# q of the first chunk, one token tile at a time

## The chip, the cores and the metric

The kernel runs on one core of a Trainium2 chip. The metric is the device time of one execution in microseconds (us). The core's engines each run their own queue of instructions in order and wait for one another through semaphores: TensorE (matmuls, and transposes as matmuls with an identity), VectorE, ScalarE, GpSimd, and SyncE (SP), which here only starts transfers. ScalarE and GpSimd can start transfers too. In the profile these are PE (weight loads apart, as PEld), DVE, ACT, POOL and SP; L284 is line 284 of the kernel.

## What is computed

One block of a transformer on x (2048 tokens, 1024 features): h = x + attention(layernorm(x)), then h2 = h + gated MLP(layernorm(h)). The change lies in the first projection of the first 512 tokens. Cut to it:

```
qkv = (layernorm(x) @ wqkv).reshape(B, S, 3, H, Dh)      # H = 32 heads of Dh = 32
logits = einsum('bhsd,bhswd->bhsw', q, kg) * scale       # 8 keys per token, 2 apart
o = einsum('bhsw,bhswd->bhsd', softmax(logits), vg)
h = x + o @ wo
h2 = h + B(layernorm(h))                                 # gelu, spatial mixing over all tokens, w_out
```

The layernorm has no learned scale: (x - mean) / sqrt(var + 1e-5), over the features of a token.

## The kernel before

The 2048 tokens are cut into 4 chunks of 512, and a chunk into 4 token tiles of 128 (one token per partition). Chunk 0 begins the kernel. Its tiles' statistics come from VectorE (`stats`, `stats_half`: two bn_stats of 512 columns and a bn_aggr) or, for tile 3, from two summing passes on ScalarE (`sums_act`, `var_act`). ScalarE takes the root, VectorE the reciprocal, and `norm` writes the normalised tile `xn`. TensorE transposes it in 8 blocks of 128x128 (`xpose`), because a matmul needs the features on the partitions, and two copies (`xput`) bring the transposed tile from PSUM, the accumulation memory, into `xnT[0]`. For tiles 0 and 2 the copies are ScalarE's, for 1 and 3 VectorE's.

The q projection multiplies `wqs`, the 1024x1024 weights of q, with `xnT[0]`. The contraction over 1024 features is cut into 8 slices (kt), the 1024 outputs into 8 groups of 128 (dl). `wqs` is seen with the dl index innermost, so the 128 weight columns of one dl lie 8 elements apart in memory; the same holds for k and v (`wk`, `wv`, L433), not for the weights of later stages (`win`, L790). Before, tiles 0 and 1 go together through q: for dl 0 to 3, all kt, 32 matmuls of 256 columns (`q_left`; 24 of them before the transposes of tiles 2 and 3, 8 after). Then tiles 2 and 3 do the same for dl 0 to 3, 32 matmuls of 256 columns; then all four tiles go through dl 4 to 7, 32 matmuls of 512 columns. All 96 are on L284. `q_out` copies finished accumulators into `att_in[0][0]`, from which attention reads q.

TensorE's clock is at half speed at first. Before any data is there, TensorE runs `NWARM` = 20 matmuls on zeros (L209).

PSUM holds three `acc` buffers and one `L` buffer. Transposed tiles 0 and 2 go through `L`, as do the warm-ups; 1 and 3 go through `acc`.

Transfers of the start: SP issues half of x0 and half of x1 (tiles 0 and 1), ScalarE the other halves, then SP all of x2 and ScalarE all of x3. GpSimd issues `csb`, the constants with the identity that the transposes need (104 KB). Then SP issues the 8 slices of wq (256 KB each), two pairs of x tiles for chunk 1, wk, x for chunks 2 and 3, and wv.

In this part of the kernel each engine's order is the order of the source, written by hand. The rest (k and v of chunk 0, the layernorm of chunks 1 to 3, attention, MLP) is ordered by a list planner, `Order`. It is given a cost in us for each operation and, in `Order({...})`, the time at which each engine is taken to become free after the hand-written part; it decides in which order operations are issued, not when. `G` keeps its operations. The planner's items on "DMA" with fixed times (17.5 for the sums of tile 7, 26.2 for q) stand for times at which something is taken to be ready.

After q, TensorE's next work is k of chunk 0 (L433), 64 matmuls of 512 columns, then v, and then it is filled by projections of later chunks while VectorE does attention.

Of the kernel before, what the change touches and what calls it, by code (L numbers as in the profile page):

```python
# [10 lines left out]
FP32 = mybir.dt.float32  # L11
BF16 = mybir.dt.bfloat16
# [8 lines left out]
P = 128  # L21
# [8 lines left out]
EPS = 1e-5  # L30
SCALE = DH ** -0.5
NEG = -1.0e9
NWARM = 20
XRB = 3
LMODE = (1, 1, 1, 1)
LSLACK, BSLACK = 2.0, 2.0
# [89 lines left out]
def kernel(  # L126
# [28 lines left out]

    cpool = ctx.enter_context(tc.tile_pool(name="consts", bufs=1))
    csb = cpool.tile([P, 416], BF16, name="csb")
    dma_w(csb[:], consts_d.ap()[:, :])
    ident = csb[:, 0:128]
    E32 = csb[:, 128:160]  # L160
    B4 = csb[:, 160:288]
# [17 lines left out]
    def new_acc():  # L179
        return ps_acc.tile([P, 2, CH], FP32, name="acc", tag="acc")  # L180
# [19 lines left out]
    def load_pair(k):  # L200
        x_slot(2 * k)
        x_slot(2 * k + 1)
        dma(pairs[k][:], x2d[2 * k * P:(2 * k + 2) * P, :].rearrange("(t p) d -> p t d", p=P))
# [10 lines left out]
    with tc.manual_schedule(engines={mybir.EngineType.SP}):  # L214
        for i in range(TPC):
            x_slot(i)
        for i in range(2):
            for q_, lo in ((nc.sync, 0), (nc.scalar, CH)):
                q_.dma_start(xts[i][:, lo:lo + CH], x2d[i * P:(i + 1) * P, lo:lo + CH])
        dma(xts[2], x2d[2 * P:3 * P, :])  # L220
        A.dma_start(xts[3], x2d[3 * P:4 * P, :])
        for kt in range(KT):
            dma(wsb[0][:, kt, :], wq_view[:, kt, 0:D])
        load_pair(2)
        load_pair(3)
        dma(wsb[1][:], wq_view[:, :, D:2 * D])
        load_pair(4)
        load_pair(5)
        xl = att.tile([P, TPC, D], BF16, name="xl", tag="prod", bufs=2)
        dma(xl[:], x2d[3 * CH:4 * CH, :].rearrange("(t p) d -> p t d", p=P))  # L230
        for i in range(TPC):
            xts[3 * TPC + i] = xl[:, i, :]
        dma(wsb[2][:], wq_view[:, :, 2 * D:3 * D])
# [4 lines left out]
        eng.bn_stats(st[:, 1, :], xts[i][:, 512:1024])  # L238
        V.bn_aggr(mv1[:, i, :], st[:])

    def stats_half(i, hf, st=None):
        if hf == 0:
            st = l1.tile([P, 2, 6], FP32, name="bnst", tag="bnst")
        V.bn_stats(st[:, hf, :], xts[i][:, hf * CH:(hf + 1) * CH])
        if hf:
            V.bn_aggr(mv1[:, i, :], st[:])
        return st

    def sums_act(i, k, junk, sm=None):
        if k == 0:  # L250
            sm = l1.tile([P, 4], FP32, name="sm", tag="sm")
        A.activation(junk, xts[i], (ACTF.Identity, ACTF.Square)[k], accum_out=sm[:, k:k + 1])
        return sm
# [6 lines left out]
    def root(lo, hi):  # L260
        sd = l1.tile([P, TPC], FP32, name="sd1", tag="sd1")
        A.activation(sd[:, 0:hi - lo], mv1[:, lo:hi, 1], ACTF.Sqrt, bias=eps_t[:])
        return sd

    def norm(i, out=None):
        xn = l1.tile([P, D], BF16, name="xn", tag="xn", bufs=4)[:] if out is None else out
        V.tensor_scalar(xn, xts[i], mv1[:, i, 0:1], rstd1[:, i:i + 1], op0=ALU.subtract, op1=ALU.mult)
        return xn

    xnT[0] = xtp.tile([P, TPC, KT, P], BF16, name="xnT", tag="xnT")  # L270

    xns = {c: bp.tile([P, TPC, D], BF16, name=f"xns{c}", tag=f"hn{c - 1}", bufs=1) for c in (1, 2)}

    def xpose(i, xn):
        tps[i] = ps_acc.tile([P, 2, 2 * CH], BF16, name="tpb", tag="acc") if i % 2 else ps_att.tile([P, 2, 2 * CH], BF16, name="tpa", tag="L")
        for a in range(KT):
            T.transpose(tps[i][:, a // 4, (a % 4) * P:(a % 4 + 1) * P], xn[:, a * P:(a + 1) * P], ident)  # L277

    def xput(i):
        for hf in range(2):  # L280
            (V.tensor_copy if i % 2 else A.copy)(xnT[0][:, i, 4 * hf:4 * hf + 4, :], tps[i][:, hf, 0:CH].rearrange("p (a s) -> p a s", a=4))  # L281

    def q_mm(dl, kt, lo, hi):
        T.matmul(qacc[dl // 2][:, dl % 2, lo * P:hi * P].rearrange("p (a b) -> p a b", b=P), wqs[:, kt, dl, :], xnT[0][:, lo:hi, kt, :],  # L284
                 start=(kt == 0), stop=(kt == KT - 1))

    def q_left(lo, hi):
        for kt in range(lo, hi):
            for dl in range(4):
                q_mm(dl, kt, 0, 2)  # L290

    def q_out(dp):
        A.copy(att_in[0][0][:, 2 * dp:2 * dp + 2, :], qacc[dp][:])

    att_in = {}

# [5 lines left out]
        alloc_att_in(0, which)  # L302
    V.memset(att_in[0][1][:, :, 0:HALO], 0.0)
    V.memset(att_in[0][2][:, :, 0:HALO], 0.0)
    tps, qacc = {}, {}
    wqs = wsb[0][:].rearrange("p kt (m dl) -> p kt dl m", dl=DLO)

    def junk():
        return l1.tile([P, D], BF16, name="jk", tag="xn", bufs=4)[:]

    wsq = l1.tile([P, 1], FP32, name="wsq", tag="wsq")
    A.activation(wsq[:], eps_t[:], ACTF.Sqrt)
    stats(V, 0)
    sd0 = root(0, 1)
    stats(V, 1)
    sd1 = root(1, 2)
    sm = sums_act(3, 0, junk())
    V.reciprocal(rstd1[:, 0:1], sd0[:, 0:1])
    xn = {0: norm(0)}
    V.reciprocal(rstd1[:, 1:2], sd1[:, 0:1])  # L320
    xn[1] = norm(1)
    xpose(0, xn[0])
    xput(0)
    st2 = stats_half(2, 0)
    xpose(1, xn[1])
    xput(1)
    stats_half(2, 1, st2)
    sums_act(3, 1, junk(), sm)
    sd2 = root(2, 3)
    var_act(3, sm)  # L330
    sd3 = root(3, 4)
    V.reciprocal(rstd1[:, 2:3], sd2[:, 0:1])
    xn[2] = norm(2)
    V.reciprocal(rstd1[:, 3:4], sd3[:, 0:1])
    xn[3] = norm(3)
    qacc[0], qacc[1] = new_acc(), new_acc()
    q_left(0, 6)
    xpose(2, xn[2])
    xput(2)
    xpose(3, xn[3])  # L340
    xput(3)
    q_left(6, KT)
    sm7 = sums_act(7, 0, junk())
    sums_act(7, 1, junk(), sm7)
    for dp in range(2):
        for dl in (2 * dp, 2 * dp + 1):
            for kt in range(KT):
                q_mm(dl, kt, 2, TPC)
        q_out(dp)
    for dp in (2, 3):  # L350
        qacc[dp] = new_acc()
        for dl in (2 * dp, 2 * dp + 1):
            for kt in range(KT):
                q_mm(dl, kt, 0, TPC)
        q_out(dp)
    wo_sb = wtile([P, DLO, D], "wo_sb", "wB")
    win_view = B_w_in.rearrange("(kt p) n -> p kt n", p=P)
    win_specs = [(FH, 1024), (FH + 1024, 768), (0, 1024), (1024, 768)]
# [4 lines left out]
        dma_w(t[:], win_view[:, :, c0:c0 + wd])  # L363
        wins[k] = t

    o_ = Order({"PE": 24.9, "ACT": 26.0, "DVE": 14.4, "POOL": 12.0}, {"acc": 3, "L": 1, "prod": 1, "part": 2, "xn": 4})
    add = o_.add
    G = {}

# [8 lines left out]
    def ln1(c):  # L378
        sts = []
        for il in range(TPC):  # L380
            i = c * TPC + il
            arrive = add("DMA", X_AT[c] + 0.8 * il, lambda: None)
            if il < TPC - 1 or c == 3:
                sts.append(add("DVE", 1.4, lambda i=i: stats(V, i), [arrive], prio=LNPRIO[c]))
                continue
            if c == 1:
                G["sm", c] = sm7
                sa = add("DMA", 17.5, lambda: None)
            else:
                def sums(i=i):  # L390
                    G["sm", c] = sums_act(i, 0, junk())
                    sums_act(i, 1, junk(), G["sm", c])
                sa = add("ACT", 2.4, sums, [arrive], prio=4.0, lat=0.2)
            sts.append(add("DVE", 0.45, lambda i=i: var_act(i, G["sm", c]), [sa], prio=LNPRIO[c]))
        def ve():
            G["ve", c] = l1.tile([P, TPC], FP32, name="ve1", tag="ve1")
            V.tensor_scalar(G["ve", c][:], mv1[:, c * TPC:(c + 1) * TPC, 1], EPS, None, op0=ALU.add)
        s1 = add("DVE", 0.15, ve, sts, prio=LNPRIO[c] - 0.5)
        r1 = add("POOL", 1.05, lambda: nc.gpsimd.tensor_tensor(rstd1[:, c * TPC:(c + 1) * TPC], G["ve", c][:], nhalf[:], op=ALU.pow),
                 [s1], lat=0.4)  # L400
        def nrm(il):
            if c == 3 and il == 0:
                xns[c] = bp.tile([P, TPC, D], BF16, name="xns3", tag="hn0", bufs=1)
            norm(c * TPC + il, xns[c][:, il, :])
        ns = [add("DVE", 0.48, lambda il=il: nrm(il), [r1] + ([G["xnT", 1]] if c == 3 else []), prio=LNPRIO[c] - 0.5,
                  free="prod" if c == 3 and il == TPC - 1 else None) for il in range(TPC)]
        G["normed", c] = ns[-1]
        def tr():
            xnT[c] = xtp.tile([P, TPC, KT, P], BF16, name="xnT", tag="xnT")
            i_ = nc.sync.dma_start_transpose(xnT[c][:].rearrange("p il a s -> p (il a) s"), xns[c][:].rearrange("s il (a p) -> s (il a) p", p=P))  # L410
            if c == 3:
                tc.add_manual_dep(i_.ins, G["vload", 1].ins.name, wait_for, reason="keep the xbar transpose out of the sums and loads")
        G["xnT", c] = dma_op(9.0, tr, ns + ([G["qkvlast", c - 2]] if c >= 2 else []))
# [40 lines left out]

    def attention(c):
        if c == 0:
            d_q = add("DMA", 26.2, lambda: None)
            d_k, d_v = G["ev", 0, 1, 3], G["ev", 0, 2, 3]
        else:
            def ld(which):  # L460
# [486 lines left out]
```

## Time and profile before

| | us |
|---|---|
| median of 3 runs | 727.18 (726.68 to 727.5) |
| the profiled execution | 727.23 |
| its span in the profile | 725.4 |
| TensorE busy in the span | 718.2 |
| first k matmul starts | 24.97 |
| first copy of tile 0 into xnT starts | 9.33 |
| VectorE's first work for chunk 1 starts | 14.77 |
| first product of attention (VectorE) starts | 40.03 |

The profile's span begins with the first instruction and ends with the last; the time of an execution has some 1.8 us around it. "Busy" of TensorE counts pipelined matmuls whose ends are modelled: a matmul of 512 columns shows 379 ns, but the next starts 216 ns after it. Where the starts of matmuls matter, they are read from the timeline. The granted clock of the profile's row PEclk is 9 (90% or more) in all of its 40 slices, but the profile's warm-up matmuls follow each other at 0.427 us until 6.72 us and at 0.216 us from 6.97 us on, so that the change of speed is read from them.

### The profile page before, as it was taken

To read this page: it belongs to the slowest core of one execution; us is meant where nothing else is said; L and a number is where in the kernel's file an instruction comes from. 1 tells how busy PE (TensorE), PEld (TensorE's weight loads), DVE (VectorE), ACT (ScalarE), POOL (GpSimd) and SP (SyncE) were. 2 spreads that over 40 slices of the span, in tenths; PEclk is the share of its full clock that TensorE was granted. 3 is DMA by queue.
4 is the path that set the end of the run, shared out by engine and by line. 5 is a ranking of instruction groups with operands and counts; after the bars stand their busy time and mean duration, and the time that the engine had idled before them with its cause. 6 is when DMAs were issued, how large, how long until landed. Compare 5 with 4: busy or idle time off the path is not lost.

```text
span 725.4 us, 8425 instructions
## 1 busy us (share of the span) xinstructions
PE 718.2 (99%) x3445; PEld 369.1 (51%) x3490; DVE 420.1 (58%) x467; ACT 224.7 (31%) x278; POOL 54.0 (7%) x62
## 2 busy tenths in 40 slices
PE   8999999999999999999999999999999999999998
PEld 6666665666545444444444444444444444444444
DVE  6899899989999899989940102222222222222222
ACT  4422522534338864769735520000000000000000
POOL 0100010112110110201203100000000000000000
PEclk9999999999999999999999999999999999999999
DMA  8955598488993594372759799254115311020002
GB/s 306 335 169 121 168 215 209 126 233 238 270 339 59 169 210 162 112 223 51 191 135 291 218 298 284 70 109 139 44 44 130 117 44 43 30 88 14 1 16 72
DMA packets 114614, 110.49 MB, mean 152 GB/s; under 512 B 67632, under 2 KB 92112, under 8 KB 114448
## 3 DMA queue, kind: packets, MB, share of 16 engines
q1 hardware_dynamic: 105504, 72.63, 35.2%
q0 software_dynamic: 8496, 36.74, 17.8%
q10 hardware_dynamic: 576, 0.59, 0.2%
q8 instruction: 27, 0.44, 0.2%
q14 instruction: 11, 0.09, 0.0%
HBM read 55.09 MB, written 30.74 MB: 118 GB/s over the span
## 4 chain that ended last, share of the span: by engine, by line
PE 99%; issue 0%; DVE 0%
PE acc L886 27%; PE acc L433 21%; PE acc L790 13%; PE acc L740 13%; PE acc L901 13%; PE acc L667 8%; PE acc L284 2%; PE wps L209 1%; PE pb L576 0%; PE L L521 0%; PE tpa L277 0%; PE tpb L277 0%; DVE xnT L281 0%; DVE ot L915 0%; DVE warm L206 0%
## 5 line engine op out<-in xcount | busy, mean ns | idle before, releaser
L886 PE MATMUL acc<-wspT,z2sb 128*128 128x512 bf16 x878 | 193.1, 379 | 0.9
L886 PEld LDWEIGHTS <-z2sb 128*128 128x128 bf16 x896 | 87.7, 98 | 105.7
L889 DVE TENSOR_TENSOR g<-acc,bB 128x1024 bf16<-128x1024 f32 x28 | 34.3, 1224 | 160.1 <-PE acc L886 128.2
L740 PE MATMUL acc<-win,hnT 128*128 128x512 bf16 (+1 forms) x500 | 97.7, 352 | 0.6
L790 PE MATMUL acc<-hnT,win 128*128 128x512 bf16 x448 | 98.0, 379 | 0.0
L740 PEld LDWEIGHTS <-hnT 128*128 128x128 bf16 x512 | 49.8, 98 | 47.6 <-issue 0.9
L491 DVE TENSOR_TENSOR prod<-qT,kT 128x4096 bf16<-128x4096 bf16 x32 | 72.6, 2286 | 0.5 <-ACT kT L439 0.5
L901 PEld LDWEIGHTS <-zg 128*128 128x128 bf16 x462 | 45.2, 98 | 51.7
L790 PEld LDWEIGHTS <-win 128*128 128x128 bf16 x448 | 43.6, 98 | 52.6 <-issue 0.9
L908 DVE TENSOR_TENSOR ot<-acc,hr 128x1024 bf16<-128x1024 f32 x15 | 18.4, 1225 | 69.4 <-PE acc L901 60.5
L901 PE MATMUL acc<-wout_a,zg 128*128 128x512 bf16 (+1 forms) x260 | 58.0, 372 | 0.3
L444 ACT CAST stg<-acc 128x1024 bf16<-128x1024 f32 x36 | 36.4, 1012 | 70.1 <-PE acc L433 62.2
L433 PE MATMUL acc<-xnT,wk 128*128 128x512 bf16 x256 | 56.5, 379 | 0.0
L433 PE MATMUL acc<-xnT,wv 128*128 128x512 bf16 x256 | 56.3, 379 | 0.0
L667 PE MATMUL acc<-wo_sb,av_oT 128*128 128x512 bf16 x250 | 55.6, 379 | 0.3
L433 PEld LDWEIGHTS <-wk 128*128 128x128 bf16 x256 | 36.5, 144 | 19.0 <-issue 0.7
L433 PEld LDWEIGHTS <-wv 128*128 128x128 bf16 x256 | 36.6, 144 | 18.7 <-issue 0.5
L901 PE MATMUL acc<-wout_b,zg 128*128 128x512 bf16 (+1 forms) x193 | 43.8, 372 | 0.2
L433 PE MATMUL acc<-xnT,wq 128*128 128x512 bf16 x192 | 42.4, 380 | 0.0
L667 PEld LDWEIGHTS <-av_oT 128*128 128x128 bf16 x256 | 25.0, 98 | 30.1
L495 DVE TENSOR_TENSOR prod<-prod 128x2048 bf16<-128x2048 bf16 x32 | 38.5, 1220 | 0.0
L747 ACT ACTIVATE u<-acc 128x1024 bf16<-128x1024 f32 (+1 forms) x32 | 29.3, 916 | 29.0 <-PE acc L740 28.7
(142 smaller groups left out, 573.8 us busy)
## 6 DMA issues: line engine op xcount, KB each, us to landing
qkv_d<-stg SPq DMA_DIRECT2D x36, 256.0 KB, 3.5
z_d<-z1s SPq DMA_DIRECT2D x28, 256.0 KB, 2.6
z1c<-z_d SPq DMA_DIRECT2D x28, 256.0 KB, 3.1
z_d<-u SPq DMA_DIRECT2D x12, 448.0 KB, 3.2
z2sb<-z_d POOLq DMA_DIRECT2D x12, 448.0 KB, 10.2
xr<-in_A_x_dram SPq DMA_DIRECT2D x16, 256.0 KB, 2.7
av_y<-av_z POOLq DMA_DIRECT2D x4, 1024.0 KB, 9.2
av_oT<-av_zz POOLq DMA_DIRECT2D x4, 1024.0 KB, 12.0
```

What stands on the lines that cost most here:

```text
L433: T.matmul(G[key][:, j, :].rearrange("p (a b) -> p a b", a=TPC), wv[:, kt, dl, :], xnT[c][:, :, kt, :], start=(kt == 0), stop=(kt == KT - 1))
L444: A.copy(stg[:], G[key][:])
L491: V.tensor_tensor(st["prod"][:], qT[:], kT[:, :, o:o + CH], op=ALU.mult)
L495: V.tensor_tensor(dst, p_[:, 0:4, :], p_[:, 4:8, :], op=ALU.add)
L667: T.matmul(st["acc", il][:, nh, :], oTs[c][:, dl, il * P:(il + 1) * P], wo_sb[:, dl, nh * CH:(nh + 1) * CH], start=(dl == 0), stop=(dl == ...
L740: T.matmul(accf[:, n0:n1], hnTs[c][:, il, kt, :], wins[hf][:, kt, n0:n1], start=(kt == 0), stop=(kt == KT - 1))
L747: A.activation(st["u", il][:, hf * 1024:hf * 1024 + wd], G["accz", c, il, hf][:].rearrange("p a b -> p (a b)")[:, 0:wd], ACTF.Gelu_apprx_t ...
L790: T.matmul(G["accy", c, fp][:, j, :].rearrange("p (a b) -> p a b", a=TPC), wt[:, kt, f0 * P:(f0 + 1) * P], hnTs[c][:, :, kt, :], start=(kt ...
L886: T.matmul(acc[:, j, :], z2sb[a][:, f * P:(f + 1) * P], wspT[:, a, :], start=(a == 0), stop=(a == NT - 1))
L889: V.tensor_tensor(g1[:], acc[:], bB[:, c * CH:(c + 1) * CH].unsqueeze(1).to_broadcast([P, 2, CH]), op=ALU.add)
L901: T.matmul(outs, zg[:, f, il * P:(il + 1) * P], wt[:, f0, lo:hi], start=(f == 0), stop=(f == NF - 1))
L908: V.tensor_tensor(ot[:], acc[:].rearrange("p a b -> p (a b)"), hr[:], op=ALU.add)
```

## The change

Chunk 0's q is cut by token tile. Tile 0 goes alone through all 8 slices and all 8 dl (64 matmuls of 128 columns, `q_tile(0, ...)`), tile 1 the same (64), and then tiles 2 and 3 together (64 matmuls of 256 columns in two halves of four dl). Transposes and copies are issued by half tiles (4 blocks). The copies of tiles 0 and 1 are ScalarE's, those of 2 and 3 VectorE's. The two halves of tile 0 use an `acc` and the `L` buffer, tile 1 an `acc`, tiles 2 and 3 `L`. Statistics of all four tiles are VectorE's, each tile with its own root, reciprocal and norm in turn; tile 0's norm is made in two halves. x2 and x3 are issued by SP behind wq slices 3 and 5. `csb` is issued by ScalarE, between its halves of x0 and x1. There are 14 warm-up matmuls, not 20. Four times given to the planner are changed, and one more by 0.1.

```diff
-NWARM = 20
+NWARM = 14
...
-    dma_w(csb[:], consts_d.ap()[:, :])
...
         for i in range(2):
             for q_, lo in ((nc.sync, 0), (nc.scalar, CH)):
                 q_.dma_start(xts[i][:, lo:lo + CH], x2d[i * P:(i + 1) * P, lo:lo + CH])
-        dma(xts[2], x2d[2 * P:3 * P, :])
-        A.dma_start(xts[3], x2d[3 * P:4 * P, :])
+            if i == 0:
+                A.dma_start(csb[:], consts_d.ap()[:, :])
         for kt in range(KT):
             dma(wsb[0][:, kt, :], wq_view[:, kt, 0:D])
+            if kt in (3, 5):
+                i = 2 + kt // 4
+                dma(xts[i], x2d[i * P:(i + 1) * P, :])
...
+    def tp_tile(in_l):
+        pool, tag = (ps_att, "L") if in_l else (ps_acc, "acc")
+        return pool.tile([P, 2, 2 * CH], BF16, name="tp" + tag, tag=tag)
+
+    def xpose(i, hf, ps):
+        for a in range(4):
+            T.transpose(ps[:, hf, a * P:(a + 1) * P], xn[i][:, (4 * hf + a) * P:(4 * hf + a + 1) * P], ident)
+
+    def xput(i, hf, ps, cp):
+        cp(xnT[0][:, i, 4 * hf:4 * hf + 4, :], ps[:, hf, 0:CH].rearrange("p (a s) -> p a s", a=4))
+
+    def q_mm(dst, dl, kt, lo, hi, first=True, last=True):
+        T.matmul(dst.rearrange("p (a b) -> p a b", b=P), wqs[:, kt, dl, :], xnT[0][:, lo:hi, kt, :],
+                 start=(first and kt == 0), stop=(last and kt == KT - 1))
+
+    def q_tile(i, lo, hi):
+        if lo == 0:
+            qacc[i] = new_acc()
         for kt in range(lo, hi):
-            for dl in range(4):
-                q_mm(dl, kt, 0, 2)
+            for dl in range(DLO):
+                q_mm(qacc[i][:, dl // 4, (dl % 4) * P:(dl % 4 + 1) * P], dl, kt, i, i + 1, dl % 4 == 0, dl % 4 == 3)
+
+    def q_tile_out(i):
+        A.copy(att_in[0][0][:, :, i * P:(i + 1) * P], qacc[i][:].rearrange("p a (d s) -> p (a d) s", d=4))
...
+    def scale(i):
+        sd = root(i, i + 1)
+        V.reciprocal(rstd1[:, i:i + 1], sd[:, 0:1])
...
     stats(V, 0)
+    scale(0)
+    xn[0] = norm(0, parts=2)
+    tpa, tpl = tp_tile(False), tp_tile(True)
+    xpose(0, 0, tpa)
+    xput(0, 0, tpa, A.copy)
+    xpose(0, 1, tpl)
+    xput(0, 1, tpl, A.copy)
     stats(V, 1)
+    scale(1)
     xn[1] = norm(1)
+    q_tile(0, 0, 4)
+    tp = tp_tile(False)
+    xpose(1, 0, tp)
+    xpose(1, 1, tp)
+    q_tile(0, 4, 6)
+    xput(1, 0, tp, A.copy)
+    stats(V, 2)
+    scale(2)
     xn[2] = norm(2)
+    xput(1, 1, tp, A.copy)
+    q_tile(1, 0, 4)
+    stats(V, 3)
+    scale(3)
     xn[3] = norm(3)
+    tp = tp_tile(True)
+    xpose(2, 0, tp)
+    xpose(2, 1, tp)
+    xput(2, 0, tp, V.tensor_copy)
+    xput(2, 1, tp, V.tensor_copy)
+    q_tile(0, 6, KT)
+    q_tile_out(0)
+    tp = tp_tile(True)
+    xpose(3, 0, tp)
+    xpose(3, 1, tp)
+    xput(3, 0, tp, V.tensor_copy)
+    xput(3, 1, tp, V.tensor_copy)
+    q_tile(1, 4, KT)
     sm7 = sums_act(7, 0, junk())
+    q_tile_out(1)
     sums_act(7, 1, junk(), sm7)
+    for half in range(2):
+        acc = new_acc()
+        for j in range(4):
             for kt in range(KT):
+                q_mm(acc[:, j // 2, (j % 2) * 2 * P:(j % 2 + 1) * 2 * P], 4 * half + j, kt, 2, TPC)
+        A.copy(att_in[0][0][:, 4 * half:4 * half + 4, 2 * P:CH], acc[:].rearrange("p a (d s) -> p (a d) s", d=2))
...
-    o_ = Order({"PE": 24.9, "ACT": 26.0, "DVE": 14.4, "POOL": 12.0}, {"acc": 3, "L": 1, "prod": 1, "part": 2, "xn": 4})
+    o_ = Order({"PE": 22.4, "ACT": 23.6, "DVE": 14.5, "POOL": 12.0}, {"acc": 3, "L": 1, "prod": 1, "part": 2, "xn": 4})
...
-                sa = add("DMA", 17.5, lambda: None)
+                sa = add("DMA", 17.8, lambda: None)
...
-            d_q = add("DMA", 26.2, lambda: None)
+            d_q = add("DMA", 23.9, lambda: None)
```

## The prediction

> **What bounds the kernel.** I read the page's totals first, then the chain of waits in order of time, then the waits of TensorE alone. The totals (busy us, share of the span, instructions):
>
> ```profile
> PE 718.2 (99%) x3445; PEld 369.1 (51%) x3490; DVE 420.1 (58%) x467; ACT 224.7 (31%) x278; POOL 54.0 (7%) x62
> ```
>
> The chain (start, length, what):
>
> ```profile
> 1.19 7.25 PE wps L209 x20
> 8.45 0.04 issue
> 8.49 0.61 PE tpa L277 x8
> 9.09 0.46 PE tpb L277 x8
> ...
> 9.58 0.43 DVE xnT L281
> ...
> 10.15 2.81 PE acc L284 x24
> 12.96 0.45 PE tpa L277 x8
> 13.41 0.45 PE tpb L277 x8
> 13.85 11.28 PE acc L284 x72
> 25.14 50.07 PE acc L433 x232
> ```
>
> The waits of TensorE that are not for the warm-ups, all of them (sum, times, longest):
>
> ```profile
> PE acc L284 <- DVE xnT L281: 0.6, 1, 0.6
> ```
>
> TensorE works without a break from 10.15 us to the end; the chain behind 25.14 holds nothing but its matmuls and 0.05 us gaps. So what the change is worth is the moment at which the first k matmul (L433) starts: 24.97 us by the timeline. Up to there TensorE has 20 warm-ups (until 8.45), 32 transposes, a 0.6 us wait for the copies into xnT, and q.
>
> Two further views give the prices. The groups by shape in two very short stretches, each at a point where other matmuls had emptied the weight path: wk (columns 8 elements apart), then win (columns side by side).
>
> ```profile
> L433 PE MATMUL acc<-xnT,wk 128*128 128x512 bf16 x1 | 0.4, 439 | 0.0
> L433 PEld LDWEIGHTS <-wk 128*128 128x128 bf16 x1 | 0.1, 145 | 0.4 <-issue 0.4
> ```
>
> ```profile
> L790 PE MATMUL acc<-hnT,win 128*128 128x512 bf16 x1 | 0.4, 389 | 0.0
> L790 PEld LDWEIGHTS <-win 128*128 128x128 bf16 x1 | 0.1, 95 | 0.4 <-issue 0.4
> ```
>
> An undisturbed matmul of this shape shows 379 ns. The one whose load was not hidden shows 389 with side-by-side weights and 439 with strided ones: the strided load costs 60 ns (64 from its own start) before columns can flow. wq is read with the same stride.
>
> The timeline of VectorE and ScalarE gives one token tile's normalisation:
>
> ```profile
> 3.24 0.70 DVE L237 BATCH_NORM_STATS2 bnst<-xp 128x6 f32<-128x512 bf16 x1 [1.93 <-DMA xp<-in_A_x_dram]
> 3.85 0.68 DVE L238 BATCH_NORM_STATS2 bnst<-xp 128x6 f32<-128x512 bf16 x1
> 4.56 0.21 DVE L239 BATCH_NORM_AGGREGATE mv<-bnst 128x2 f32<-128x12 f32 x1
> 4.80 0.30 ACT L262 ACTIVATE sd<-mv,eps_t 128x1 f32<-128x1 f32 x1 [1.15 <-DVE mv L239]
> ...
> 12.31 0.16 DVE L334 RECIPROCAL rstd<-sd 128x1 f32<-128x1 f32 x1
> 12.51 0.55 DVE L267 TENSOR_SCALAR xn<-xp,mv,rstd 128x1024 bf16<-128x1024 bf16 x1
> ```
>
> Statistics 1.53 us (3.24 to 4.77), root 0.33, reciprocal and norm 0.75: some 2.6 us a tile, the next able to begin 0.1 sooner.
>
> **Start.** Fourteen warm-ups: the weight loads of the warm-ups come every 0.427 us until 6.72, then faster, so the fourteenth starts at 6.72 and TensorE is free at 6.97. Before, the first transposes went into the warm-ups' own L buffer and waited for its last write, to 8.49; now they go into an acc buffer. Tile 0's transposes need csb, moved from GpSimd's queue to ScalarE's ahead of x1's half. Before, csb landed at 7.0 (issued 1.23, 5.8 to landing) and x1 at 5.2; I take csb under 5.5, hidden by the warm-ups, and x1 up to 0.5 later, hidden below. Tile 0's norm is ready at 5.6 (4.77 + 0.33 + 0.2 + half of 0.55), also hidden. First four transposes 6.97 to 7.19 (0.056 each, 0.45 per 8), the copy on ScalarE 7.40 to 7.98 (0.58), 0.14 for the semaphore as before: q starts at 8.12, not 10.15: **-2.03**; but tile 1's 8 transposes, done by then before, come later: **+0.45**. Slice 0 of wq landed at 8.7 (2.13 + 6.6), slice 7 at 13.4 (8.64 + 4.8), 0.67 apart. x2 and x3 no longer lie ahead, so slice 0 comes by 7.4 at equal bytes, and no slice is waited for.
>
> **Matmuls of tiles 0 and 1.** 64 matmuls of 256 columns at 0.109 us become 128 of 128 columns. (0.109: the 72 in 11.28 us hold 32 of 512 at 0.216.) No row has 128 columns with strided weights. Lower bound: 0.056, the transposes, whose loads are side by side. Upper: 0.109, the 256-column spacing, under which the same load is already hidden. If each load begins as the preceding matmul starts, a matmul can follow every max(0.056, 0.064) us, and I take 0.065. 128 x 0.065 - 64 x 0.109 = 8.32 - 6.98 = **+1.34** (bounds +0.2 and +7.0). The Trainium skill's page "TensorE: Matmul & The Clock Gate", section "Back-to-back issue gap", gives some 81 ns for each matmul in a stream of load and matmul pairs at 128 columns; by it the term would be an estimated +3.4. The trace's transposes at 56 ns do not follow it. Tiles 2 and 3: 32 of 512 at 0.216 become 64 of 256: 6.98 - 6.91 = **+0.07**.
>
> **VectorE.** x3's statistics come over from ScalarE (+1.5), and four copies stand where two tiles' copies stood. The root of tile 1 is queued on ScalarE behind both copies of tile 0 (second ends 8.46): root 8.42 to 8.72, norm 1 to 9.5, in time for tile 1's transposes at 10.2. Here x1's delay is covered by 1 us. Then x2's statistics 9.41 to 10.94; the root waits behind tile 1's first copy (10.64 to 11.22), so 11.43; norm 2 at 12.2; x3's statistics to 13.65, norm 3 to 14.76; tile 2's copies 14.67 to 15.42. They free the one L buffer that tile 3's transposes need: 15.56. TensorE's side: 32 matmuls 8.12 to 10.2, transposes 10.65, 16 to 11.7, 32 to 13.78, transposes 14.23, 16 to 15.27. So it stands for 15.56 - 15.27 = **+0.3**. Behind it: transposes to 16.0, 32 to 18.1, 64 x 0.109 to 25.07.
>
> x2's landing: wq slice 2 had the same bytes ahead, 10.1; but between 5.2 and 8.1 the 616 KB of csb, x2 and x3 took 2.9 us where the later rate (256 KB in 0.67) makes 1.6, and without csb on the slow queue up to 1.25 may go: 8.85. Middle 9.5, 0.1 past 9.41: **+0.1** (bounds 0 and +0.65).
>
> **Sum**: -2.03 + 0.45 + 1.34 + 0.07 + 0.3 + 0.1 = +0.2. The profiled execution took 727.23 us, its span 725.4; the median is 727.18. Forecast 727.4.
>
> What else moves is hidden: ScalarE issues three transfers as before. GpSimd loses one. SP's queue has x2 and x3 behind slices 3 and 5, and wk, which landed at 21.9, is not needed before 25. VectorE starts chunk 1's statistics about 2.2 later (17.0, was 14.77); behind it are the statistics of chunks 2 and 3 and the first attention product (40.03). Small idle times (0.4, 0.5, 0.5) leave that product about 0.8 late; the matmul that first needs the result (75.14) stands 0.8 behind it, so TensorE waits 0 to 0.3. The hand-set clocks only reorder later work; engines and true starts shift by like amounts (TensorE 2.7, VectorE 2.5 behind the list), so I cost this at nothing, between -0.5 and +0.5.
>
> **Rivals.**
> *Faster, 726.2.* The clock rises early, csb's slow stretch vanishes and 128 columns run at 0.056. Then VectorE alone sets the third transposes: with q from 7 us, norm 1 at 8.5 and x2 at 8.85, tile 2's copies end near 14.7 and k starts near 14.8 + 0.45 + 32 x 0.056 + 6.98 = 24.0, 1.0 sooner. For it: csb's slow stretch. Against: 439 to 389. Four tiles of 2.55 behind x0 at 3.24, copies, and that tail give 23.7 as the earliest, so 0.2% needs luck besides.
> *Slower: the strided load decides, 729.8.* Place: loads of q_tile. If a load cannot start as the preceding matmul does, the spacing lies between 0.065 and 0.109; at the middle, 0.087, k starts at 8.12 + 24 x 0.056 + 128 x 0.087 + 6.98 = 27.6, 2.6 late. It decides from 0.078 (26.4); at 0.109 the time is 732.6. For it: loads show 143 ns against 98. Against: the matmul flowed 60 ns after such a load. The skill's 81 ns (same page and section) would be an estimated 729.1.
> *Clock not yet granted, 728.5.* Thirteen warm-ups ran slow; fourteen leave a margin of one. If the rise comes after them, 32 matmuls run at 0.107: 32 x 0.042 = +1.35, less the 0.3 stand, on top of 0.2. Against: before, the rise came inside the fourteen. The same page, section "What's actually happening", calls the clock's window free-running, so that the rise shifts from run to run; one profile cannot show it.
>
> **Numbers.** Forecast 0.55, faster rival 0.22, strided load 0.15, clock 0.08. Differences under 0.2% (1.45 us) count as none. The forecast puts 0.50 there, 0.01 below and 0.04 above; the faster case 0.09 and 0.13 below; the load 0.02 and 0.13 above; the clock 0.03 and 0.05 above. Sum: faster 0.14, same 0.64, slower 0.22. The range goes from the faster case's far side (k at 23.3) to the load's middle: 725.6 to 729.8; the forecast's own is 726.5 to 728.3.
>
> **What would show it.** Right: first transposes near 7.0, q from 8.1, q_tile matmuls 0.065 apart, a short wait of tile 3's transposes for VectorE's copies, first k matmul at 25.2. Spacing of 0.056 or 0.08 speaks for the first or second rival; warm-up loads 0.427 apart to the end, for the third. Wrong altogether: a new TensorE wait after 25 us, or k before 23.7.

## The result and the profile after

| | before | after |
|---|---|---|
| median, 20 runs of each on one chip (us) | 726.77 (726.12 to 727.5) | 728.13 (727.72 to 728.61) |
| ratio after to before | | 1.0019, 95% interval 1.0012 to 1.0026 |
| the profiled execution | 727.23 | 728.24 |
| its span | 725.4 | 726.4 |
| first k matmul starts | 24.97 | 24.81 |
| first k matmul to first matmul of the spatial mixing (L886, now L894) | 407.15 | 407.88 |
| last store's landing to the end of the span | 0.91 | 1.36 |

The kernel became 1.36 us slower, 0.19%, which is just inside the 0.2% called no change; the interval reaches to both sides of that bound. It is still told apart from zero. The last three rows say where the time went, and none of it is in the front that was rewritten: k starts 0.16 *sooner*, then 0.73 is lost somewhere in the 400 us that follow, and 0.45 behind the last store. -0.16 + 0.73 + 0.45 = 1.02, the difference of the two spans (1.0) and of the two profiled executions (1.01). The other 0.35 up to the medians is spread: the profiled execution of the kernel before lies 0.46 above its median and has a late k (24.97; two other kernels with the same front, below, show 24.82 and 24.35).

By the totals TensorE is busy for 720.4 us, 99% of the span, so it still has no slack. The chain of waits in order of time, up to the first k matmul (start, length, what):

```profile
1.19 5.79 PE wps L208 x14
6.98 0.24 PE tpacc L276 x4
7.22 0.02 issue
7.24 0.59 ACT xnT L279
7.84 0.04 issue
7.88 2.10 PE acc L282 x32
9.98 0.46 PE tpacc L276 x8
...
14.17 0.55 DVE xn L263
14.71 0.67 DVE xnT L279 x2
15.39 0.05 issue
15.44 0.62 PE tpL L276 x8
16.05 8.92 PE acc L282 x96
24.98 51.80 PE acc L441 x240
```

Here the reader sees the prediction's picture of the front: warm-ups, four transposes, the copy, q from 7.88, and then VectorE's row of norms and copies, which sets tile 3's transposes at 15.44. The waits of TensorE, all but that of the warm-ups (sum, times, longest):

```profile
PE tpL L276 <- DVE xnT L279: 0.6, 1, 0.6
PE acc L282 <- ACT xnT L279: 0.5, 1, 0.5
PE pb L584 <- ACT AB L589: 0.4, 1, 0.4
```

The first two belong to the front. The third is new and lies at 252 us, 227 us behind the rewritten front, in the part that the planner orders. The timeline of TensorE there, before and then after (start, length, line, operation, count, and in brackets the idle time before it and what ended it):

```profile
250.53 0.39 PE L576 MATMUL pb<-attn,csb 32*128 32x512 bf16 x2
250.54 0.39 PE L576 MATMUL pba<-attn,csb 32*128 32x512 bf16 x2
250.86 2.33 PE L790 MATMUL acc<-hnT,win 128*128 128x512 bf16 x10
```

```profile
251.22 0.39 PE L584 MATMUL pba<-attn,csb 32*128 32x512 bf16 x2
252.01 0.39 PE L584 MATMUL pb<-attn,csb 32*128 32x512 bf16 x2 [0.40 <-ACT AB L589]
252.34 1.90 PE L798 MATMUL acc<-hnT,win 128*128 128x512 bf16 x8
```

`pb` and `pba` spread the attention weights over partitions, two matmuls each with 32 rows. Before, the two pairs start 0.01 apart and the next matmul follows after 0.33: they run side by side. After, `pba` is issued first, and `pb` alone 0.79 later, with 0.33 to the next: `pb` goes into the one L buffer, and that is freed only when ScalarE's copy AB ends. The copy is late because of what stands ahead of it on ScalarE, whose timeline follows for both, before first:

```profile
240.11 1.87 ACT L769 ACTIVATE u<-u,l3nb,l3rstd 128x1792 bf16<-128x1792 bf16 x1
242.00 1.28 ACT L542 ACT_TABLE_LOAD   x1
243.30 1.15 ACT L542 ACTIVATE sme<-sme 128x512 f32<-128x512 f32 x2
...
247.94 1.01 ACT L581 CAST AB<-pb 128x1024 bf16<-128x1024 f32 x1 [0.16 <-PE pba L576]
248.84 1.89 ACT L769 ACTIVATE u<-u,l3nb,l3rstd 128x1792 bf16<-128x1792 bf16 x1
```

```profile
239.94 3.64 ACT L777 ACTIVATE u<-u,l3nb,l3rstd 128x1792 bf16<-128x1792 bf16 x2
243.60 1.28 ACT L550 ACT_TABLE_LOAD   x1
244.89 1.15 ACT L550 ACTIVATE sme<-sme 128x512 f32<-128x512 f32 x2
...
249.18 1.88 ACT L777 ACTIVATE u<-u,l3nb,l3rstd 128x1792 bf16<-128x1792 bf16 x1
250.95 1.01 ACT L589 CAST AB<-pb 128x1024 bf16<-128x1024 f32 x1
```

After, two normalisations of `u` stand in the queue ahead of the table load for the exponential where one stood before. So the exponential begins at 244.89, not 243.30, and all that hangs on it comes later. That is 1.6 of the 3.0 us by which the first copy AB is later (250.95, was 247.94). The rest is one more normalisation of `u`: it followed the copy before (248.84) and precedes it after (249.18). No operation was added; the order of the issued instructions changed. What can have changed it is the hand-set times given to `Order`.

The third loss is behind the last store. The DMA issues at the end, before and after:

```profile
722.89 0.33 SPq L916 DMA_DIRECT2D out_dram<-ot  x1
```

```profile
723.46 0.33 SPq L924 DMA_DIRECT2D out_dram<-ot  x1
```

Both transfers take the same time to land, 1.56 and 1.57 us from their issue (724.45 and 725.03). But the span ends 0.91 behind that landing before, and 1.36 after. SP's last waits, taken from the trace, show why:

```
before: 723.27 723.33 723.40 723.47 723.53 723.59 723.65 723.71 | landing 724.45 | 724.47
after:  723.85 | landing 725.03 | 725.04 725.11 725.18 725.24 725.30 725.36 725.42 725.48
```

At the end of the kernel SP checks the counters of its finished transfers one after another, about 0.062 us each. Before, eight checks are done ahead of the landing and the last store's own counter comes last. After, the last store's counter is checked early, and seven more checks stand behind it: 7 x 0.063 = 0.44. The transfers that SP and ScalarE issue use eight counters in turn. With `csb` taken from GpSimd, those two issue one more (ScalarE has `csb` for x3, and SP has x3 besides): by the trace 209, where 208 were whole turns of eight. So the last store falls on the next counter, which is the first of them and not the last.

### The profile page after: what moved, and what is told of

Read it like the earlier page. It is cut to its first block, busy times and chain, and to the rows that moved or that the text cites. A ratio compares the mean times of both kernels' runs of the same rounds, so it can differ in the third digit from the quotient of the medians.

```text
span 726.4 us, 8645 instructions
## 1 busy us (share of the span) xinstructions
PE 720.4 (99%) x3580; PEld 371.9 (51%) x3580; DVE 420.7 (58%) x468; ACT 222.0 (31%) x274; POOL 52.3 (7%) x61
## 4 chain that ended last, share of the span: by engine, by line
PE 97%; ACT 2%; DVE 1%; issue 0%; DVEq 0%; ACTq 0%
PE acc L894 27%; PE acc L441 21%; PE acc L748 13%; PE acc L909 13%; PE acc L798 12%; PE acc L675 8%; PE acc L282 2%; PE wps L208 1%; ACT u L777 1%; ACT z1s L804 0%; PE pb L584 0%; PE L L529 0%; ACT L550 0%; DVE xn L263 0%; ACT AB L589 0%
## 5 line engine op out<-in xcount | busy, mean ns | idle before, releaser
L894 PE MATMUL acc<-wspT,z2sb 128*128 128x512 bf16 x896 | 194.0, 379 | 0.0
L894 PEld LDWEIGHTS <-z2sb 128*128 128x128 bf16 x896 | 87.7, 98 | 105.7
L804 ACT ACTIVATE z1s<-acc 128x1024 bf16<-128x1024 f32 x28 | 28.5, 1023 | 35.0 <-PE acc L798 33.4
```

What stands on the lines that cost most here:

```text
L804: A.activation(z1s[:], G["accy", c, fp][:], ACTF.Gelu_apprx_tanh)
L894: T.matmul(acc[:, j, :], z2sb[a][:, f * P:(f + 1) * P], wspT[:, a, :], start=(a == 0), stop=(a == NT - 1))
```

## The experiments

The two theories for the lost time were these. **List and tail**: the front gains or loses almost nothing; the new times in `Order` cost some 0.7 by another order near 250 us, and the one transfer more on SP and ScalarE costs 0.44 at the end. **Front**: the loss lies in the 128-column matmuls, the strided loads or VectorE's longer row, and what shows at 250 us and at the end is covered. Beside the medians, each result is split as in the table above: start of k, length from there to the mixing, and length behind the last store.

**Old times in the list.** The changed kernel, with the planner's times as before:

```diff
-Order({"PE": 22.4, "ACT": 23.6, "DVE": 14.5, ...
+Order({"PE": 24.9, "ACT": 26.0, "DVE": 14.4, ...
-add("DMA", 17.8, ...)      add("DMA", 23.9, ...)
+add("DMA", 17.5, ...)      add("DMA", 26.2, ...)
```

> The changed kernel with the planner's old times (TensorE 24.9, ScalarE 26.0, VectorE 14.4, sums 17.5, q 26.2); its list behind q is then the one of before. Theory A (a part of the loss is the new list: the place near 250 us where two broadcast matmuls wait for a ScalarE copy and run one after the other, 0.78 us): some 0.8 us faster than the changed kernel, about 727.3 beside 726.8 for before; the two broadcast pairs of chunk 2 run together and the 0.5 us gap between them is gone. Rival B (the loss is in the front, which in most executions is slower than the profile shows): no faster than 728.1.

Measured: k at 24.90, 407.19 to the mixing, 1.34 behind the store; 727.65 (726.79 to 728.73) against 726.98 of the kernel before, timed beside it, ratio 1.0010 (1.0001 to 1.0019). So the difference to the kernel before falls from 1.36 to 0.67. All but 0.04 of the loss of 0.73 is gone and the pair runs side by side again, by the timeline of TensorE:

```profile
250.51 0.39 PE L584 MATMUL pb<-attn,csb 32*128 32x512 bf16 x2
250.52 0.39 PE L584 MATMUL pba<-attn,csb 32*128 32x512 bf16 x2
```

**New times in the kernel before.** The same edit the other way round, with nothing else changed.

> The kernel before with the planner's new times and nothing else. Theory A: 0.8 us slower than before, about 727.6, with the same wait near 250 us. Rival B: as before, 726.8. Rival C (the new list hurts only where the front's true times differ from it): no wait there, no loss.

Measured: k at 24.82, 407.89, 0.92; 727.82 against 726.98, ratio 1.0013 (1.0004 to 1.0022). The old front with the new times has the whole loss, and the new wait:

```profile
251.24 0.39 PE L576 MATMUL pba<-attn,csb 32*128 32x512 bf16 x2
252.03 0.39 PE L576 MATMUL pb<-attn,csb 32*128 32x512 bf16 x2 [0.40 <-ACT AB L581]
```

So five numbers that describe the front, and not the front itself, cost 0.74 us.

**The counter of the last store.** The load of the bias row `bB`, needed only late, is cut into eight transfers, seven more, in the changed kernel. With the one that the change added these are eight, a full turn of the counters.

```diff
-    dma(bB[:], B_b_sp.unsqueeze(0).to_broadcast([P, S]))
+    for k in range(8):
+        dma(bB[:, k * S // 8:(k + 1) * S // 8],
+            B_b_sp[k * S // 8:(k + 1) * S // 8].unsqueeze(0).to_broadcast([P, S // 8]))
```

> The changed kernel with the load of the bias rows cut into 8 transfers, so that SP and ScalarE issue 7 more in all and the last store falls on the counter that is checked last, as before. Theory A (0.44 us of the loss are the checks that still stand behind the last store): from the landing of the last store to the end of the span about 0.85 us instead of 1.3, and about 727.7. Rival B: 728.1.

Measured: 24.76, 407.89, **0.90**; 727.53 (727.29 to 728.14) against 726.98, ratio 1.0010 (1.0001 to 1.0018). The span behind the landing is that of the kernel before. The kernel before with `bB` in two transfers, one more, is the converse:

> The kernel before with the load of the bias rows cut into 2 transfers, one more than before, as the change has one more. Theory A: 0.45 us slower than before, about 727.2, all of it behind the last store. Rival B: 726.8.

Measured: 24.35, 407.14, **1.34**; 727.20 against 726.98, ratio 1.0006 (0.9997 to 1.0014). In the profiles the tail comes and goes with the number of transfers as expected. The timed ratio alone doesn't show it: 0.44 us is 0.06%, and the interval is three times as wide.

**Tile 3's transposes in an `acc` buffer.** This takes away the stand at 15.44, which came from the L buffer.

```diff
     q_tile_out(0)
-    tp = tp_tile(True)
+    tp = tp_tile(False)
```

> The changed kernel with tile 3's transposes in an acc buffer instead of L, so that they don't wait for VectorE's copies of tile 2. Theory A (the k start of 24.8 is set by VectorE's chain of four tiles and the wait for L, not by the clock's rise): tile 3's transposes at 14.9 instead of 15.4, right behind q's last slices of tile 0, and the first k matmul at 24.3. Rival B (the weight loads set it): as now, 24.8.

Measured in one execution: k at 24.44, 407.89, 1.36; 727.89. TensorE's timeline shows no wait ahead of the transposes (the second line):

```profile
13.87 1.18 PE L282 MATMUL acc<-xnT,wq 128*128 128x128 bf16 x16
15.00 0.62 PE L276 MATMUL tpacc<-csb,xn 128*128 128x128 bf16 x8
```

In the changed kernel they started at 15.44: 0.44 gained there, 0.37 of it left at k.

**Weights side by side.** `wqs` is seen so that the 128 columns of one dl lie next to each other. Which columns make a dl is thereby different: q comes out in another order of its columns.

```diff
-    wqs = wsb[0][:].rearrange("p kt (m dl) -> p kt dl m", dl=DLO)
+    wqs = wsb[0][:].rearrange("p kt (dl m) -> p kt dl m", dl=DLO)
```

> The changed kernel with wq of chunk 0 read with side-by-side columns (dl outermost), so that q's columns of this chunk come in another order. Theory A (the strided load takes 64 ns and sets the spacing of 128-column matmuls): the first 32 q matmuls 0.056 us apart, 1.8 us in all instead of 2.1; but the third and fourth transposes still wait for VectorE, so k starts only some 0.3 sooner, about 24.5. Rival B (the spacing comes from something else, such as the writes to PSUM): 0.065 as now.

Measured in one execution: k at 24.77, 407.89, 1.36; 728.20. The weight loads of q by shape, changed kernel first (count | sum in us, mean ns of one | idle):

```profile
L282 PEld LDWEIGHTS <-wq 128*128 128x128 bf16 x191 | 15.0, 145 | 0.5 <-issue 0.5
```

```profile
L282 PEld LDWEIGHTS <-wq 128*128 128x128 bf16 x191 | 13.4, 98 | 1.5 <-issue 0.6 <-DMA wq<-in_A_wqkv_dram 0.2
```

And the timeline of TensorE around the first 32 matmuls, again the changed kernel first:

```profile
7.88 2.10 PE L282 MATMUL acc<-xnT,wq 128*128 128x128 bf16 x32 [0.45 <-ACT xnT L279]
9.82 0.61 PE L276 MATMUL tpacc<-csb,xn 128*128 128x128 bf16 x8
...
15.44 0.62 PE L276 MATMUL tpL<-csb,xn 128*128 128x128 bf16 x8 [0.56 <-DVE xnT L279]
```

```profile
7.87 1.95 PE L282 MATMUL acc<-xnT,wq 128*128 128x128 bf16 x32 [0.45 <-ACT xnT L279]
9.66 0.61 PE L276 MATMUL tpacc<-csb,xn 128*128 128x128 bf16 x8
...
15.54 0.62 PE L276 MATMUL tpL<-csb,xn 128*128 128x128 bf16 x8 [0.99 <-DVE xnT L279]
```

Strided, 32 matmuls of 128 columns take 9.82 - 7.88 = 1.94, 0.061 each; side by side 1.79, 0.056. So the stride costs 5 ns a matmul, 0.6 for all 128. What TensorE saves by 15.5 is not gained: the wait grows from 0.56 to 0.99, since VectorE sets the transposes of tile 3. In this execution VectorE also waited 0.16 for x2, which landed at 9.42. Only the 0.14 saved behind them counts, less the 0.10 by which they came later. The expectation of an earlier k missed for that reason.

**All of it undone.** The changed front with tile 3 in `acc`, the old times in the list and `bB` in eight transfers.

> The changed kernel with the planner's old times, the 7 extra transfers and tile 3's transposes in acc: what is left is the front alone, without its stand. Theory A: k at 24.3, 407.15 from there to the mixing stage, 0.9 behind the last store: 726.4, a little under before (726.9). Rival B (something of the front reaches further): over 727.

Measured: 24.34, 407.15, 0.90; 726.62 (725.89 to 727.02) against 726.64, ratio 0.9998 (0.9989 to 1.0007). Both side effects are away, and the rewritten front, without its stand at 15.44, is worth nothing that can be measured: the interval goes from 0.8 us faster to 0.5 slower.

**Warm-ups.** The kernel before with `NWARM` 14 shows what the fewer warm-ups do without the new front; the changed kernel with 20 asks the converse.

> The kernel before with 14 warm-ups and nothing else. Theory A (20 warm-ups are longer than needed, by more the later the clock rises): transposes at 7.2 to 7.3, when csb and xn are there, k at 23.7 to 23.9 and 726.1 to 726.3, faster than before and than the change. Rival B (14 don't get the clock up in time): q runs partly at 0.107 to 0.21 us a matmul and the time is 726.8 or more.

Measured: k at 24.08 (23.7 to 23.9 was expected), 407.15, 0.92; 726.28 against 726.64, ratio 0.9994 (0.9985 to 1.0003). The old front with that one number changed starts k sooner here than the new front in any of its five profiles (24.27 to 24.99). TensorE's timeline:

```profile
1.19 5.52 PE L209 MATMUL wps<-warm 128*128 128x512 bf16 x14 [1.19 <-DVE eps_t L210]
7.15 0.62 PE L277 MATMUL tpa<-csb,xn 128*128 128x128 bf16 x8 [0.44 <-DVE xn L267]
```

Repeated:

> The kernel before with 14 warm-ups, once more. Theory A: 0.3 to 0.7 us faster than before, with the first k matmul near 24.1. Rival B (the first result was chance): no difference.

Measured: 24.57, 407.13, 0.92; 726.49 against 726.84, ratio 0.9996 (0.9987 to 1.0005). k is later than the first time; 13 warm-ups were slow here and 11 there. Twice some 0.35 below, and neither interval is clear of 1: likely a small gain, not shown.

> The changed kernel with 20 warm-ups. Theory A (with 14, VectorE sets the k start and TensorE has slack; with 20, TensorE starts 1 to 1.5 later and becomes the bound): transposes at 7.9 to 8.5, q at 9 to 9.6, k at 25.6 to 26.2. Rival B (VectorE keeps the bound): k at 24.8 all the same.

Measured in one execution: k at 25.36, 407.89, 1.36; 728.79. In its profile the clock rose after 7 slow warm-ups, so that 20 of them were over by 7.13, only 0.31 later than 14 in the changed kernel, where 12 were slow. k is later for another reason: x2 landed at 9.81, VectorE began its statistics at 9.84 (9.21 in the changed kernel), and TensorE still waited 0.72 for the copies that follow. So VectorE keeps the bound here, as in rival B. What 20 cost when the clock rises late was not seen.

**True times in the list.** The planner was told 22.4 for the end of TensorE's hand-written part, and k really starts at 24.8. First that one number alone:

```diff
-Order({"PE": 22.4, ...
+Order({"PE": 24.8, ...
```

> The changed kernel with one number changed: the planner is told that TensorE becomes free at 24.8, where the trace has it, not at 22.4. Theory A (this one number turns the order near 250 us): 407.15 us from the first k matmul to the mixing stage instead of 407.88. Rival B (the other four times matter too): 407.88 or something between.

Measured in one execution: 24.99, 407.64, 1.36; 728.41. The pair near 250 us runs side by side again, but another wait appears 11 us earlier, by the timeline of TensorE:

```profile
239.81 0.40 PE L529 MATMUL L<-part,csb 128*32 128x512 bf16 x4 [0.32 <-DVE part L509]
```

So 407.64 speaks for rival B: the other times matter too. The planner, run by itself on these times, issues the same order as with the old times but for nine places on VectorE, all of them in the layernorms of later chunks, and ScalarE's 23.6 alone turns these nine. VectorE's last `part` starts at 239.33 here and at 238.80 with the old times.

Then all five by what the profile shows (TensorE 24.8, ScalarE 26.0, VectorE 16.8, sums 20.1, q 26.1):

> The changed kernel with all five of the planner's times set to what the trace of the changed kernel shows (TensorE 24.8, ScalarE 26.0, VectorE 16.8, sums 20.1, q 26.1). Theory A (the 0.74 us came from a list made for times 2.4 too early): 407.15 from the first k matmul to the mixing stage, no wait of TensorE behind 25 us, about 727.4. Rival B (VectorE's 2 us are late whatever the list says): a wait of TensorE for VectorE remains and the time is 727.9 or more.

Measured: 24.27, 407.15, 1.36; 727.76 (726.98 to 728.39) against 726.72, ratio 1.0013 (1.0004 to 1.0023). Its profiled execution, 727.18, has no wait behind the front. But the median is 0.6 above that, though the loss in the list is gone from the profile. The runs spread over 1.4 us, those with the old times over 1.9, against 0.9 for the changed kernel with its own times. A list without a wait in one profile may have one in other executions, such as the list with 24.8 alone had. That is only argued (the kernel before spreads over 1.4 too). Another candidate is the front: with it k started at 24.27 in this profile and up to 24.99 in others. No profile of a longer execution was taken, and why true times gave no better median stays open.

## Why the prediction was right, point by point

The forecast was 727.4 with k 0.2 later; 728.13 was measured, inside the range. Against the kernel before that is +1.36 where +0.2 was forecast, at the upper edge of what counts as no change (1.45). The reasons were partly others than those predicted.

- **Start.** First transposes predicted at 6.97, measured 6.82; q from 8.12, measured 7.88. `csb` landed at 3.99, x1's half at 6.14 (0.4 later than allowed, hidden as said: the statistics of that half began at 6.99). Right.
- **128-column matmuls, +1.34.** Mechanism right, size too large. The forecast's 0.065 was 0.061 in the first 32 and 0.063 over the 48 of the next stretch, so that the term is 128 x 0.062 - 6.98 = +0.96. The strided load does cost something in each matmul: 61 ns against 56 with side-by-side weights, and the load itself shows 145 against 98. The 81 ns of the Trainium skill's page "TensorE: Matmul & The Clock Gate", section "Back-to-back issue gap", are borne out by neither. The Trainium skill's page "SBUF — State Buffer", section "Door 1: The DMA port swizzle", has SBUF read in lines of 16 bytes, which are 8 bf16 elements, and a crossing to a new line pays. The longer load agrees with that; that the lines are its reason was not tested.
- **The stand of tile 3's transposes, +0.3.** 0.56 measured. VectorE's side was nearly exact (copies of tile 2 end at 15.38, predicted 15.42; transposes 15.44, predicted 15.56); TensorE came there at 14.88, not 15.27: 0.24 of that is the earlier start of q, the rest the shorter matmuls. These errors cancel: time saved before 15.4 becomes waiting, as the kernel with side-by-side weights shows.
- **x2's landing, +0.1.** 9.0, where 9.5 was taken: nothing was lost to it in the profiled execution; x2's statistics began at 9.21, behind tile 1's norm. In other profiles of this front the term is there. With x2 landed at 9.18 (`bB` in eight transfers), 9.39 (old times), 9.48 (24.8 alone) and 9.81 (20 warm-ups), its statistics began 0.02 to 0.03 later each time.
- **k.** 25.2 predicted, 24.81 measured. In five profiles of kernels with the changed front as it is, k starts between 24.27 and 24.99, in three with the old front and 20 warm-ups between 24.35 and 24.97. So the old and new front differ by less than one execution differs from the next. What sets k is not the same, though. In the three old ones k starts 14.8 behind the start of q, and q follows the rise of the clock: it starts at 10.15, 9.99 and 9.52 after 13, 12 and 10 slow warm-ups. In the five new ones k starts 10.2 behind VectorE's first copy of tile 2 (14.05 to 14.80), whether 6 or 12 warm-ups were slow. The gain at the start (2) is given back to 128-column matmuls, to the transposes of tile 1 and to VectorE: -2.27 + 0.45 + 0.96 + 0.07 + 0.56 = -0.23 by the measured terms (0.07 as predicted), beside -0.16 for k.
- **What failed: "The hand-set clocks only reorder later work; ... so I cost this at nothing, between -0.5 and +0.5."** It is the largest single loss, +0.74, outside its own bounds. The argument was that engines and true starts shift by like amounts. In the changed kernel they do: TensorE comes 2.4 behind its time in the list (24.81, 22.4) and VectorE 2.3 (16.77, 14.5). But that protects nothing. The same list costs 0.74 under the old front, where the two come 2.4 and -0.1 behind it, and the old list costs 0.04 under the new front, where they come 0.0 and 2.5 behind. So the cost is that of the order in the list, not of a mismatch between engines. The planner, run by itself with one time changed at a time, shows that TensorE's number alone turns the orders of TensorE and ScalarE and that the other four turn neither. It does so in jumps: with 22.9 for TensorE the planner keeps TensorE's old order, with 23.4 it does not, and from 23.9 on it does.
- **What was not in the sum: the end.** The transfers were counted queue by queue ("ScalarE issues three transfers as before ... GpSimd loses one"), and that SP thereby has one more was given no price. It moved the last store to a counter that is checked earlier: +0.44.
- **Rivals.** The faster one needed 0.056 in every matmul and csb's slow stretch gone. The second came true; VectorE still set k at 24.8, not 24.0. The strided load stayed far under 0.078. The clock's rise came after 12 slow warm-ups, in time. With 14 it was close: in two other profiles (tile 3 in `acc`, and the kernel before with 14 repeated) all 13 intervals between warm-ups were slow, and the first transposes behind them already ran at 0.056. The earliest k that the prediction gives the faster rival, 23.7, comes to 23.4 by its own terms (3.24 + 4 x 2.55 + 0.75 + 0.45 + 1.79 + 6.98); nothing hangs on it.

The prediction named "a new TensorE wait after 25 us" as what would prove it wrong. It is there. That the number held is partly luck: the losses in two places that the sum put at nothing, or did not have, were still smaller than what counts as a change, and the range was wide enough for them.

## What to carry to other kernels

A list planner with hand-set times has those times as part of the code: whoever moves the front must check the order that comes out 200 us later, and one number, lowered by 2.5 us where k moved by 0.16, cost 0.74 here. Look for a change's cost in three stretches, up to the last place where its own order ends, from there to the last matmul, and behind the last store: a queue with one transfer more can lengthen the last. And before a front is rewritten around a resource, try its smallest part: the old kernel with 14 warm-ups instead of 20 was the fastest measured (ratios 0.9994 and 0.9996, not clear of 1).

## What the hardware showed that was not expected

**The clock's rise moves by as much as the whole effect.** Counted by the spacing of the warm-ups (0.427 slow, 0.216 fast), it came after 6 to 13 slow ones in 14 profiles, which is 2.6 to 5.5 us after the first. Two examples, the changed kernel (12 slow) and the one with all true times (6 slow), same 14 warm-ups, by the timeline of TensorE:

```profile
1.19 5.79 PE L208 MATMUL wps<-warm 128*128 128x512 bf16 x14 [1.19 <-DVE eps_t L209]
6.82 0.39 PE L276 MATMUL tpacc<-csb,xn 128*128 128x128 bf16 x4
```

```profile
1.19 4.53 PE L208 MATMUL wps<-warm 128*128 128x512 bf16 x14 [1.19 <-DVE eps_t L209]
6.03 0.40 PE L276 MATMUL tpacc<-csb,xn 128*128 128x128 bf16 x4 [0.31 <-DVE xn L263]
```

With the early rise TensorE waits for the norm (0.31), with the late one for its own warm-ups. The Trainium skill's page "TensorE: Matmul & The Clock Gate", section "What's actually happening", calls the window free-running and some 3.4 us long, by which the rise shifts from run to run, and has the rise after at least one busy window; the shift agrees, but 2.6 us is less than one window.

**Checks at the end have a price.** Each check of SP behind the last landing adds about 0.062 us (725.04 to 725.48 for eight). In the four kernels compared here SP checks in the order of the counters, whichever was used last, so that the same store ends the kernel 0.9 or 1.34 to 1.36 us after it landed, by which counter it fell on.

**Two pairs of 32-row matmuls ran side by side only as neighbours.** `pb` and `pba`, four matmuls with 32 rows, take 0.33 us to the next matmul when they stand next to one another with nothing to wait for. When `pb` has to wait, it takes 0.33 by itself, and from the first of the four to the next matmul it is 1.12 (251.22 to 252.34).
